# Fused local attention and gMLP on Trainium2: first row tiles remade scaled, an earlier hold in the attention, another order of output rows

## The chip, the cores and the metric

The kernel runs on one core of one Trainium2 chip. The metric is the device time of one execution in microseconds (us): the median of several runs. The engines are named as in the profile: PE is TensorE (matrix products), PEld its weight loads, DVE is VectorE, ACT is ScalarE, POOL is GpSimd, SP is SyncE, which here only issues transfers (DMAs). Each engine works through its own list of instructions in order and waits where an operand isn't ready or a buffer isn't free.

## The reference

With S = 2048 rows and D = 512 columns (batch 1):

```python
xn = layernorm(x)                                   # no scale or shift
# A: 32 heads of 16, each row attends to 8 rows: itself and 7 earlier ones, 2 apart
q, k, v = split(xn @ wqkv)
logits  = einsum(q, k at pos - 2*w for w in 0..7) / 4, masked before row 0
s       = (softmax(logits) weighted sum of v) @ wo
# B: gMLP, F = 1792, Fh = 896
z  = gelu(xn @ w_in)
z1, z2 = z[:, :Fh], layernorm(z[:, Fh:])
g  = w_sp @ z2 + b_sp[:, None]                      # w_sp: 2048 x 2048 over the rows
b  = (z1 * g) @ w_out
out = x + s * silu(b)
```

All is float32. The kernel writes each float32 operand of a product as a high and a low part and sums three products (high x high, high x low, low x high).

## The kernel before

**Layout.** Rows are dealt to NT = 16 row tiles of 128, and these to four chunks of JC = 4 tiles (512 rows). A big buffer, BIG, holds first the planes of xn turned into columns (a high and a low plane for each of four blocks of columns, k = 0 to 3, and each row tile), later z2 and the gated product. To make a high and a low part is called a split: ACT copies the high part (L195), DVE subtracts for the low one (L197).

**Order of the products on PE.** First q, k and v: three groups of columns g = 0, 1, 2 (`product`, L385 to L387), two row tiles at a time (`pair`). ACT moves each result to a staging tile (L433, tile `stage`) and issues its store to a scratch tensor, qkv_d. Then z1 with columns as rows of the result (L687 to L689, tile `z`; weights `w_5h`, `w_lasth` and so on, in the trace), with 7 blocks f by 4 chunks c; ACT applies gelu (L696, tile `z1t`) and stores it. Then z2 (L717 to L719, also tile `z`), gelu at L720 and a layernorm on DVE, POOL and ACT. Then the mixing with w_sp (L812, tile `g`), written as seven block products whose operands are sums of blocks of w_sp and of z2 (the sums L393 are formed on DVE and POOL and kept in sums_d; weights `wsp_0` to `wsp_7` are blocks of w_sp, `ws_0` to `ws_7` such sums; `tr` are transposed tiles of z2 read back from t_d). Then the products with w_out (L1054 to L1056, tile `b`) and with wo (the same lines, tile `s`), and the last arithmetic sg = s * silu(b) + x.

**The rows of the first chunk.** xn of the first four row tiles is only centred when it is put in BIG: their factor 1/std is not known so early. It is applied late: in `pair` and after z2 as the `scale` of ACT's activation (`late_rstd`, which is 1.0 for other tiles), and for z1 on DVE, where chunk c = 0 is multiplied by `rb` (L694), a tile that holds the factors as a row in all partitions. `rows_out` writes means and factors to mv_d, and rb is read from there in the middle of group g = 1, after the weights `wqkv_0` to `wqkv_3` of group 2 have been asked for.

**Raw slots.** Weights, rb and the attention's results that are read back (`ol`) pass through RAW = 4 buffers of one tag. A load into a slot waits until the operations on its last content are through.

**Attention.** It runs on DVE in 32 steps: 16 units, each of four heads (64 columns) and half of the row tiles, and per unit two steps of one chunk each, all kept in one order by `line`. A step multiplies k by q (L565, tile `pr`), sums over the head (L572, tile `lg`), for a unit shifts by the maximum (L587 to L590) and divides by the sum (L601 to L603), then weights v (L609, tile `pv`; `sums_of` lists these 32 operations), folds (L620 on POOL, in the last steps on DVE; L625, L626), transposes (L633, tile `tt`) and stores to o_d from POOL's queue. The scores run three steps ahead of the weighting. k, q and v are read from qkv_d, the first of them by SP's queue, later ones by POOL's. Attention has the lowest priority: a scheduler that lays out each engine's list when the kernel is built puts its steps between other work.

**The hold.** In `plain`, one dependency by hand keeps the weighting of the twelfth step behind the split of weight js = 4 of the first block product. It only orders DVE's list.

**The end.** `load_o` reads four row tiles of attention results for one of the groups, in four parts k, half of each by SP and half by POOL, into raw slots, and splits them (L197; the first group's parts go to BIG, later ones to `o_0` to `o_3`). A group is one chunk; the last four steps of the attention, the 29th to the 32nd, finish the chunks 0, 1, 2 and 3 in this order. The order of chunks in the product with wo is `rows_of` (1, 3, 0, 2).

Of the kernel before, what the change touches and what calls it, by code (L numbers as in the profile page):

```python
# [57 lines left out]
def kernel(  # L58
# [174 lines left out]
        hi, lo = xn_at(j)  # L233
        pin(nc.vector.tensor_tensor(lo, blocks(pt), hi.bitcast(F32), op=ALU.subtract))

    def rows_out(j0, j1):
        turned = const.tile([P, 2 * NT], F32, tag="mvt", name=f"mvt_{j0}", bufs=1)
        pin(nc.vector.transpose(turned, mvx.rearrange("p j a -> p (j a)")))
        for a in range(P // Q):
            pin(nc.sync.dma_start(  # L240
                mv_d[j0:j1, :, a * Q : (a + 1) * Q].rearrange("j a q -> (j a) q"),
                turned[a * Q + 2 * j0 : a * Q + 2 * j1],
            ))
# [51 lines left out]
    def opening(wg):  # L295
        def high(k):
            hi, lo = weight_pair(f"wqkv_0_{k}")
            pin(nc.scalar.activation(hi, raw[k], AF.Copy))
            wg[k] = hi, lo

        def low(k, eng):
            pin(eng.tensor_tensor(wg[k][1], raw[k], wg[k][0].bitcast(F32), op=ALU.subtract))

        left = [12, 12]

        def times(j, *kab):
            for k, a, b in kab:
                pin(nc.tensor.matmul(  # L308
                    first[j], xn_at(j)[a][:, k], wg[k][b],
                    start=left[j] == 12, stop=left[j] == 1,  # L310
                ))
                left[j] -= 1

        x = [load_x(0)]
        raw = [fetch(wqkv[:, 0, 0, :], GC, "wqkv_0_0")]
        x.append(load_x(1))
        raw += [fetch(wqkv[:, 0, k, :], GC, f"wqkv_0_{k}") for k in (1, 2)]
        raw.append(t35("wqkv_0_3r")[:, :GC])
        pin(nc.sync.dma_start(raw[3], wqkv[:, 0, 3, :]))
        x.append(load_x(2))  # L320
        stats_x(0, x[0])
        high(0)
        normal_x(0, x[0])
        low(0, nc.vector)
        p = turned_x(0, x[0])
        stats_x(1, x[1])
        low_x(0, p)
        high(1)
        normal_x(1, x[1])
        rstd_x(0)  # L330
# [12 lines left out]
        normal_x(2, x[2])  # L343
        rstd_x(1)
        first.append(mm("qkv_0_1"))
        times(1, *[(k, 0, 0) for k in range(KB - 1)], (0, 0, 1), (1, 0, 1))
        times(0, (3, 0, 0), (3, 1, 0), (2, 0, 1))
        p = turned_x(2, x[2])
        times(1, (3, 0, 0), *[(k, 1, 0) for k in range(KB)], (2, 0, 1))
        times(0, (3, 0, 1))  # L350
        times(1, (3, 0, 1))
        x += [load_x(j) for j in range(3, OPEN)]
        for j in range(OPEN, OPEN + 4):
            fetch_rows(j)
        raw1 = [fetch(wqkv[:, 1, k, :], GC, f"wqkv_1_{k}") for k in range(3)]
        raw1.append(t2("wqkv_1_3r", 1, tag="tz", bufs=1))
        pin(nc.sync.dma_start(raw1[3], wqkv[:, 1, 3, :]))
        for j in range(3, OPEN):
            xt = x[j]
            stats_x(j, xt)  # L360
            low_x(j - 1, p)
            normal_x(j, xt)
            if j - 1 < JC:
                rstd_x(j - 1)
            first.append(mm(f"qkv_0_{j - 1}"))
            left.append(12)
            times(j - 1, *[(k, 0, i) for i in range(2) for k in range(KB)])
            p = turned_x(j, xt)
            times(j - 1, *[(k, 1, 0) for k in range(KB)])
            row_stats(OPEN + j - 3)  # L370
        low_x(OPEN - 1, p)
        for j in range(10, 13):
            fetch_rows(j)
        for j in range(6, 10):
            fetch_cols(j)
        rows_ready(6, 9)
        rows_out(6, 9)
        return raw1

    def product(g, j, wg):  # L380
# [46 lines left out]
    def pair(g, j0):  # L427
        pins[0] = False
        stage = tmp.tile([P, 2 * GC], F32, tag="t35", name=f"stage_{g}_{j0}", bufs=3)
        sv = stage.rearrange("p (b j c) -> p b j c", b=NBLK, j=2)  # L430
        for j in (j0, j0 + 1):
            pq = first[j] if g == 0 and j < OPEN - 1 else product(g, j, wgs[g])
            nc.scalar.activation(  # L433
                sv[:, :, j % 2, :],
                pq.rearrange("p (b c) -> p b c", b=NBLK),
                AF.Copy,
                scale=late_rstd(j),
            )
        dst = qkv_d[NBLK * g : NBLK * (g + 1), PAD:, :].rearrange(
            "b (p j) c -> p b j c", j=NT  # L440
        )[:, :, j0 : j0 + 2, :]
        nc.scalar.dma_start(dst, sv)
        pins[0] = True
# [10 lines left out]
    rows_ready(9, 13)  # L454
    pair(0, 4)
    column_tile(6)
    rows_out(9, 13)
    column_tile(7)
    low_x(6, cols[6])
    for j in range(10, 12):  # L460
# [6 lines left out]
    column_tile(8)  # L467
    low_x(7, cols[7])
    fetch_cols(12)
    rows_out(13, NT)  # L470
    pair(1, 2)
    column_tile(9)
    low_x(8, cols[8])
# [4 lines left out]
    for j in range(11, NT):  # L478
        if j + 2 < NT:
            fetch_cols(j + 2)  # L480
        turned = column_tile(j)
        if j == 12:
            for i in range(HT - 2):
                pool_sums(1, i, early_tile, turned, SYNC)
        low_x(j - 1, cols[j - 1])
        if j % 2:
            pair(0, j - 5)
    low_x(NT - 1, cols[NT - 1])
    pair(0, 12)
    pair(0, 14)  # L490
    early.__exit__(None, None, None)
    pins[0] = False
    for g in range(1, NG):
        for j in range(OPEN if g == 1 else 0, NT, 2):
            if g == 1 and j == NT // 2:
                pins[0] = True
                wgs[2] = weights(2)
                rows_out(0, JC)
                rb = raws.tile([P, 512], F32, tag="raw", name="rb", bufs=RAW)
                pin(nc.sync.dma_start(  # L500
                    rb.rearrange("p (j q) -> p j q", j=JC),
                    mv_d[:JC, 1].unsqueeze(0).to_broadcast([P, JC, P]),
                ))
            pair(g, j)
            pins[0] = False

# [15 lines left out]
    def attention():  # L522
# [26 lines left out]

        def load_v(u):  # L550
            sub, h = units[u]
            vs[u] = ap_.tile([P, HWIN, CS], F32, tag="v", name=f"v_{sub}_{h}")
            queue = nc.gpsimd if u > 1 else nc.sync
            queue.dma_start(vs[u].rearrange("p r c -> p (r c)"), window(sub, 2, h))

# [94 lines left out]
        for i, (u, j0) in enumerate(steps):  # L650
            coming = steps[i + ahead] if i + ahead < len(steps) else None
            if coming:
                if not coming[1]:
                    start(coming[0])
                pr = scores(*coming)
            if part:
                finish(part)
            if not j0:
                load_v(u)
                normed(u)  # L660
            part = weighted(u, j0)
            if coming:
                heads(*coming, pr)
            first_fold(part, nc.gpsimd if coming else nc.vector)
            if j0 + NJ == NH and u + 1 < len(units):
                exponential(u + 1)
            if coming and coming[1] + NJ == NH:
                shifted(coming[0])
        finish(part)
        tc.cur_priority = saved  # L670

# [7 lines left out]
    for f in range(FB):  # L679
        pair_ = side_pair("w1_last") if f == FB - 1 else None  # L680
        wh, wl = prep(w_in1[:, f, :], KB * P, f"w1_{f}", pair_=pair_)
        for c in range(NC):
# [7 lines left out]
            if c % 2 == 0:  # L690
                zp = t4(f"z1t_{f}_{c}")
            zt = zp[:, c % 2]
            if c == 0:
                nc.vector.tensor_tensor(zt, pz, rb, op=ALU.mult)  # L694
                pz = zt
            nc.scalar.activation(zt, pz, AF.Gelu_apprx_tanh)  # L696
            if c % 2:
                nc.scalar.dma_start(z1_d[f, c - 1 : c + 1].rearrange("c p t -> p c t"), zp)
# [13 lines left out]
    def z2_half(j, h, zt):  # L712
        xh, xl = xn_at(j)
        pz = mm(f"z2_{j}_{h}")[:, : WID[h]]
        for k in range(KB):
# [1 line left out]
            nc.tensor.matmul(pz, xh[:, k], wh, start=k == 0, stop=False)  # L717
            nc.tensor.matmul(pz, xh[:, k], wl, start=False, stop=False)  # L718
            nc.tensor.matmul(pz, xl[:, k], wh, start=False, stop=k == KB - 1)  # L719
        nc.scalar.activation(zt[:, HALF[h]], pz, AF.Gelu_apprx_tanh, scale=late_rstd(j))  # L720

    def spatial_block(c, js):
        return prep(w_sp[c, js], CT, f"wsp_{c}_{js}")
# [43 lines left out]
    for i in range(HT + 2):  # L767
        if i in (1, 3):
            raw_sums(1, HT - 2 + i // 2)
        if i < HT:  # L770
            raw_z[i] = [t4(f"zt_{j}").rearrange("p i t -> p (i t)")[:, :FH] for j in (i, HT + i)]
            for h in range(2):
                for j, zt in zip((i, HT + i), raw_z[i]):
                    z2_half(j, h, zt)
                if i == HT - 1 and h == 0:
                    spatial[0, 1] = spatial_block(0, 1)
        if i == 2:
            b_a = t4("b_a")
            nc.sync.dma_start(
                b_a, b_sp[0:2, :].rearrange("c t -> (c t)").unsqueeze(0).to_broadcast([P, 2 * CT])  # L780
# [66 lines left out]
    def plain(a, c, r):  # L847
        def w(s):
            js = r * HT + s
            pair_ = spatial.get((2 * a + c, js)) or spatial_block(2 * a + c, js)  # L850
            if (a, c, js) == (0, 0, 4):
                tc.add_manual_dep(
                    sums_of[11].ins, lows[-1].ins.name, NOSYNC, reason="first weights ahead"
                )
            return pair_

# [226 lines left out]
    wos = [ut_at(1, f) for f in range(KB)]  # L1083
    for k in range(KB):
        split(*wos[k], fetch(wo[:, k, :], D, f"wo_{k}"))
    rows_of = [c * JC + jj for c in (1, 3, 0, 2) for jj in range(JC)]
    groups = [rows_of[i] // NJ for i in range(0, NT, NJ)]
    fetched = {0: fetch_pair(0)}
    os_ = [load_o(groups[0], k, ut_at(3, k)) for k in range(KB)]
# [70 lines left out]
```

## Time and profile before

| | before |
|---|---|
| time, median of 3 runs (lowest to highest) | 706.84 us (703.7 to 707.46) |
| profiled execution: its own time | 706.57 us |
| its span in the profile | 704.8 us |
| granted TensorE clock, mean | 0.993 |
| PE busy | 689.8 us, 98% |
| DVE busy | 611.2 us, 87% |
| ACT busy | 281.8 us, 40% |
| POOL busy | 224.8 us, 32% |
| chain that ended last | PE 49%, DVE 28%, DMA 11%, issue 8% |

How to read it: the span is what the profile shows of one execution, and the execution's own time has 1.8 us more. Lines such as L694 are lines of the kernel; `z1t<-z,rb` names the tile written and those read, with buffer numbers left out, so that all `z` tiles read alike. In a timeline, a row has its start, its length, engine, line and operation; the bracket at its end is the time for which the engine had been idle and what released it, as inferred from semaphores. The "granted clock" is the share of its full clock that TensorE got.

### The profile page before, as it was taken

Reading aid. Unit: us, or ns where it says so; the run is one execution under the profiler, and the core shown is the slowest. Engines: PE = TensorE matmul, PEld = TensorE weight load, DVE = VectorE, ACT = ScalarE, POOL = GpSimd, SP = SyncE. Lnnn points to the kernel's source line nnn. Section 1 sums busy time; section 2 is a strip of 40 time slices with the busy share of each in tenths; the row PEclk is TensorE's granted clock in tenths of the full one; section 3 lists DMA queues with packets and bytes.
Section 4 is the critical chain, followed back from the end, with each engine's and each line's share of the span. In section 5 each row is a group of like instructions: output and inputs, shape, how many; then the busy total and the mean of one; then the engine's idle time right before and its main releaser. Section 6 shows DMA issues by size and latency. Waiting matters only on the chain.

```text
span 704.8 us, 9222 instructions
## 1 busy us (share of the span) xinstructions
PE 689.8 (98%) x3084; PEld 574.7 (82%) x3084; DVE 611.2 (87%) x886; ACT 281.8 (40%) x458; POOL 224.8 (32%) x242
## 2 busy tenths in 40 slices
PE   8999999999989799999999999999999999999997
PEld 7888888888868688988888878888888888888886
DVE  6774288897999999899998989999999899998266
ACT  4343332331323464696544244532433353311432
POOL 3105485933333244522122311223202102542210
PEclk9999999999999899999999999999999999999999
DMA  8769999879999864448698767757758685453997
GB/s 269 257 194 342 332 361 353 272 223 373 382 371 340 343 207 154 144 147 283 211 365 329 256 231 252 256 160 259 239 169 282 199 270 204 145 169 138 245 340 281
DMA packets 102080, 182.37 MB, mean 259 GB/s; under 512 B 9168, under 2 KB 45264, under 8 KB 102032
## 3 DMA queue, kind: packets, MB, share of 16 engines
q1 hardware_dynamic: 56480, 102.14, 44.0%
q0 software_dynamic: 13824, 52.24, 21.1%
q10 hardware_dynamic: 31728, 27.40, 11.7%
q8 instruction: 24, 0.39, 0.2%
q14 instruction: 24, 0.20, 0.1%
HBM read 122.42 MB, written 59.32 MB: 258 GB/s over the span
## 4 chain that ended last, share of the span: by engine, by line
PE 49%; DVE 28%; DMA 11%; issue 8%; POOL 2%; ACT 1%; SPq 0%; DVEq 0%; ACTq 0%; POOLq 0%
PE g L812 23%; DVE pr L565 5%; DVE lg L572 4%; PE b L1054 4%; PE b L1055 4%; PE b L1056 4%; DVE pv L609 3%; PE qkv L385 2%; PE qkv L387 2%; PE qkv L386 2%; PE s L1054 2%; PE s L1056 2%; PE s L1055 2%; DVE BIG L197 2%; PE qkv L308 2%
## 5 line engine op out<-in xcount | busy, mean ns | idle before, releaser
L620 POOL TENSOR_TENSOR pv<-pv 128x1024 f32<-128x1024 f32 x29 | 70.8, 2441 | 81.7 <-DVE pv L609 81.6
L565 DVE TENSOR_TENSOR pr<-k,q 128x2048 f32<-128x2048 f32 x32 | 76.5, 2392 | 8.7 <-DMA k<-qkv_d 5.2
L609 DVE TENSOR_TENSOR pv<-v,lg 128x2048 f32<-128x2048 f32 x32 | 73.1, 2284 | 1.3 <-DMA v<-qkv_d 0.8
L572 DVE TENSOR_REDUCE lg<-pr 128x128 f32<-128x2048 f32 x32 | 72.9, 2277 | 0.1
L634 POOL DMA_DIRECT2D o_d<-tt x32 | 18.1, 566 | 157.1 <-DVE tt L633 155.0
L433 ACT ACTIVATE stage<-qkv 128x512 f32<-128x512 f32 x36 | 21.4, 595 | 50.1 <-PE qkv L387 44.7
L717 PE MATMUL z<-w_0h,BIG 128*128 128x512 f32 x64 | 26.3, 411 | 4.3 <-DVE lg L587 4.1
L794 POOL DMA_DIRECT2D ol<-o_d x32 | 17.7, 555 | 32.4 <-DVE o_1l L197 8.3
L719 PE MATMUL z<-w_0h,BIG 128*128 128x512 f32 x64 | 26.1, 410 | 0.0
L625 DVE TENSOR_TENSOR pv<-pv 128x512 f32<-128x512 f32 x32 | 24.0, 749 | 2.4 <-POOL pv L620 2.3
L718 PE MATMUL z<-w_0l,BIG 128*128 128x512 f32 x64 | 26.0, 406 | 0.0
L544 POOL DMA_DIRECT2D k<-qkv_d x13 | 7.1, 546 | 55.7 <-DVE pr L565 55.7
L280 DVE TENSOR_TENSOR xT<-xT,mr 128x512 f32<-128x512 f32 x20 | 13.8, 688 | 11.2 <-DMA mr<-mv_d 6.4
L741 ACT ACTIVATE zt<-zt,nmz,mvz 128x896 f32<-128x896 f32 x16 | 17.4, 1130 | 14.2 <-POOL nmz L735 14.1
L393 POOL TENSOR_TENSOR sb<-sa,sb 128x512 f32<-128x512 f32 x12 | 20.1, 1672 | 4.8 <-DMA sb<-in_w_sp 4.5
L719 PE MATMUL z<-w_1h,BIG 128*128 128x384 f32 x64 | 21.5, 336 | 0.0
L717 PE MATMUL z<-w_1h,BIG 128*128 128x384 f32 x64 | 21.5, 336 | 0.0
L718 PE MATMUL z<-w_1l,BIG 128*128 128x384 f32 x64 | 21.4, 335 | 0.0
L729 DVE BATCH_NORM_STATS2 zst<-zt 128x6 f32<-128x448 f32 x32 | 18.8, 604 | 2.8 <-ACT zt L720 2.8
L195 ACT ACTIVATE BIG<-zl 128x512 fp32r<-128x512 f32 x20 | 12.2, 626 | 22.4 <-DVE zl L882 22.4
L696 ACT ACTIVATE z1t<-z 128x512 f32<-128x512 f32 x21 | 12.2, 594 | 21.7 <-DMA z_d<-z1t 19.5
L812 PE MATMUL g<-ws_1h,BIG 128*128 128x512 f32 x52 | 20.4, 391 | 0.3 <-ACT ws_1h L195 0.3
(476 smaller groups left out, 2305.4 us busy)
## 6 DMA issues: line engine op xcount, KB each, us to landing
qkv_d<-stage ACTq DMA_DIRECT2D x24, 512.0 KB
v<-qkv_d POOLq DMA_DIRECT2D x14, 704.0 KB, 5.0
k<-qkv_d POOLq DMA_DIRECT2D x13, 704.0 KB, 6.4
sums_d<-sa POOLq DMA_DIRECT2D x14, 512.0 KB, 7.3
sums_d<-sb POOLq DMA_DIRECT2D x14, 512.0 KB, 7.9
z_d<-z1t ACTq DMA_DIRECT2D x14, 512.0 KB
zl<-z_d SPq DMA_DIRECT2D x12, 512.0 KB
tr<-t_d SPq DMA_DIRECT2D x12, 384.0 KB
```

The source lines that it names most:

```text
L565: line(nc.vector.tensor_tensor(pr, taps(ks[u], j0), qb.unsqueeze(1).to_broadcast([P, W, NJ * CS]), op=ALU.mult))
L572: line(nc.vector.tensor_reduce(lgs[u][:, :, j0 * HS : (j0 + NJ) * HS], pr.rearrange("p w (i d) -> p w i d", d=DH), axis=AX.X, op=ALU.add,))
L609: line(nc.vector.tensor_tensor(pv.rearrange("p w (i d) -> p w i d", d=DH), taps(vs[u], j0).rearrange("p w (i d) -> p w i d", d=DH), lgs[u] ...
L620: eng.tensor_tensor(pv[:, 0:4], pv[:, 0:4], pv[:, 4:8], op=ALU.add)
L625: line(nc.vector.tensor_tensor(pr[:, 0:2], pr[:, 0:2], pr[:, 2:4], op=ALU.add))
L717: nc.tensor.matmul(pz, xh[:, k], wh, start=k == 0, stop=False)
L718: nc.tensor.matmul(pz, xh[:, k], wl, start=False, stop=False)
L719: nc.tensor.matmul(pz, xl[:, k], wh, start=False, stop=k == KB - 1)
L812: nc.tensor.matmul(pg, z[a], w[b], start=start and i == 0, stop=stop and i == 2, skip_group_check=seeded)
L1054: nc.tensor.matmul(pp[:, cols], hi, wh, start=k == 0, stop=False)
L1055: nc.tensor.matmul(pp[:, cols], hi, wl, start=False, stop=False)
L1056: nc.tensor.matmul(pp[:, cols], lo, wh, start=False, stop=k == n - 1)
```

## The change

It has five parts.

1. **Factors out earlier.** `rows_out` takes several ranges of row tiles, and the first four tiles go out with the last three. rb is read at j = 13 of the opening loop, before the weights of group 2 are asked for.
2. **Column tiles remade.** After the last low part of xn, four new chains remake the columns of the first chunk: DVE adds high and low part, multiplies by rb, ACT copies the high part, DVE subtracts for the low part. They use raw slots (tile `xs`). From there on, the first four tiles are like the others: L694 goes, and group 2 and z2 no longer use `late_rstd`.
3. **Two loads.** The load of the bias `b_a` moves from i = 2 to i = 5 of z2's loop. The last v tile takes a buffer of tag k and is loaded when the last scores are done, before the last steps.
4. **The hold.** The tenth step is held, for weight js = 6.
5. **Output rows.** The order of chunks in the product with wo is (1, 0, 2, 3). The product with w_out keeps (1, 3, 0, 2).

```diff
@@ rows_out
-    def rows_out(j0, j1):
+    def rows_out(*spans):
...
-        for a in range(P // Q):
+        for (j0, j1), a in itertools.product(spans, range(P // Q)):
@@ pair
-                scale=late_rstd(j),
+                scale=late_rstd(j) if g < 2 else 1.0,
@@ opening
-    rows_out(13, NT)
+    rows_out((13, NT), (0, JC))
...
     for j in range(11, NT):
...
+        if j == NT - 3:
+            rb = raws.tile([P, 512], F32, tag="raw", name="rb", bufs=RAW)
+            rbv = rb.rearrange("p (j q) -> p j q", j=JC)
+            pin(nc.sync.dma_start(rbv, mv_d[:JC, 1].unsqueeze(0).to_broadcast([P, JC, P])))
...
     low_x(NT - 1, cols[NT - 1])
+    early.__exit__(None, None, None)
+
+    for k in range(KB):
+        hi, lo = [planes[:, FB - KB + k, :JC, a] for a in range(2)]
+        xs = raws.tile([P, 512], F32, tag="raw", name=f"xs_{k}", bufs=RAW)
+        xs = xs.rearrange("p (j q) -> p j q", j=JC)
+        pin(nc.vector.tensor_tensor(xs, hi.bitcast(F32), lo.bitcast(F32), op=ALU.add))
+        pin(nc.vector.tensor_tensor(xs, xs, rbv, op=ALU.mult))
+        pin(nc.scalar.activation(hi, xs, AF.Copy))
+        pin(nc.vector.tensor_tensor(lo, xs, hi.bitcast(F32), op=ALU.subtract))
     pair(0, 12)
     pair(0, 14)
-    early.__exit__(None, None, None)
...
-                rows_out(0, JC)
-                rb = raws.tile([P, 512], F32, tag="raw", name="rb", bufs=RAW)
-                pin(nc.sync.dma_start(
-                    rb.rearrange("p (j q) -> p j q", j=JC),
-                    mv_d[:JC, 1].unsqueeze(0).to_broadcast([P, JC, P]),
-                ))
@@ load_v, and the loop over the steps
-            vs[u] = ap_.tile([P, HWIN, CS], F32, tag="v", name=f"v_{sub}_{h}")
+            vs[u] = ap_.tile([P, HWIN, CS], F32, tag="k" if u == len(units) - 1 else "v", name=f"v_{sub}_{h}")
...
-                load_v(u)
+                if u < len(units) - 1:
+                    load_v(u)
...
+            if i + ahead == len(steps):
+                load_v(len(units) - 1)
@@ z1
-            if c == 0:
-                nc.vector.tensor_tensor(zt, pz, rb, op=ALU.mult)
-                pz = zt
             nc.scalar.activation(zt, pz, AF.Gelu_apprx_tanh)
@@ z2_half
-        nc.scalar.activation(zt[:, HALF[h]], pz, AF.Gelu_apprx_tanh, scale=late_rstd(j))
+        nc.scalar.activation(zt[:, HALF[h]], pz, AF.Gelu_apprx_tanh)
@@ z2's loop
-        if i == 2:
+        if i == 5:
             b_a = t4("b_a")
@@ plain
-            if (a, c, js) == (0, 0, 4):
+            if (a, c, js) == (0, 0, 6):
                 tc.add_manual_dep(
-                    sums_of[11].ins, lows[-1].ins.name, NOSYNC, reason="first weights ahead"
+                    sums_of[9].ins, lows[-1].ins.name, NOSYNC, reason="first weights ahead"
                 )
@@ the product with wo
-    rows_of = [c * JC + jj for c in (1, 3, 0, 2) for jj in range(JC)]
+    rows_of = [c * JC + jj for c in (1, 0, 2, 3) for jj in range(JC)]
```

The scheduler moves many other instructions with these. Three places show what the prediction speaks of. The first is DVE's list at the end of the opening: `xT` and BIG are column tiles of xn, `wqkv_0l` is the low part of a weight of group 2, `pr_0` the first attention operation. Before:

```order
86 L234 TENSOR_TENSOR BIG<-xT_648,BIG 128x4x128
87 L197 TENSOR_TENSOR wqkv_0l<-wqkv_0r,wqkv_0h 128x512
88 L197 TENSOR_TENSOR wqkv_1l<-wqkv_1r,wqkv_1h 128x512
89 L197 TENSOR_TENSOR wqkv_2l<-wqkv_2r,wqkv_2h 128x512
90 L197 TENSOR_TENSOR wqkv_3l<-wqkv_3r,wqkv_3h 128x512
91 L238 STREAM_TRANSPOSE mvt_838<-mvx 128x32
92 L565 TENSOR_TENSOR pr_0_1220<-k_0_1215,q_0_1216 128x2048
```

And after, in the same place (two of the four chains):

```order
86 L234 TENSOR_TENSOR BIG<-xT_652,BIG 128x4x128
87 L499 TENSOR_TENSOR xs_730<-BIG 128x512
88 L500 TENSOR_TENSOR xs_730<-xs_730,rb 128x512
89 L502 TENSOR_TENSOR BIG<-xs_730,BIG 128x4x128
90 L499 TENSOR_TENSOR xs_735<-BIG 128x512
91 L500 TENSOR_TENSOR xs_735<-xs_735,rb 128x512
92 L502 TENSOR_TENSOR BIG<-xs_735,BIG 128x4x128
```

Twelve operations come between the last low part and the splits of wqkv, and the transpose L238 is gone from here. The second place is DVE's list near the end of z1, with the last multiplication by rb (block f = 6, chunk 0). Before:

```order
239 L609 TENSOR_TENSOR pv_0_1421<-v_0_1415,lg_1351 128x2048
240 L572 TENSOR_REDUCE lg_1395<-pr_4_1408 128x8x16
241 L197 TENSOR_TENSOR wsp_0l<-wsp_0r,wsp_0h 128x512
242 L587 MEMSET lg_1395 1x8
243 L587 MEMSET lg_1395 1x16
244 L694 TENSOR_TENSOR z1t_0_2388<-z_6_0_2375,rb 128x512
```

And after:

```order
239 L197 TENSOR_TENSOR wsp_0l<-wsp_0r,wsp_0h 128x512
240 L611 TENSOR_TENSOR lg_1369<-lg_1369,sm_1435 128x256
241 L393 TENSOR_TENSOR sb_5_2296<-sa_5_2295,sb_5_2296 128x512
242 L393 TENSOR_TENSOR sa_5_2295<-sa_5_2295 128x512
243 L393 TENSOR_TENSOR sa_5_2295<-sa_5_2295,sb_5_2296 128x512
244 L617 TENSOR_TENSOR pv_0_1439<-v_0_1433,lg_1369 128x2048
245 L580 TENSOR_REDUCE lg_1413<-pr_4_1426 128x8x16
```

The multiplication is gone, and the first weight of the mixing is split ahead of the weighting of the ninth step. The third place is DVE's list at the hold. Before, the twelfth weighting (`pv`), behind the split of wsp_4; BIG<-zt is z2's split:

```order
364 L197 TENSOR_TENSOR BIG<-zt_2904,BIG 128x4x128
365 L197 TENSOR_TENSOR wsp_3l<-wsp_3r,wsp_3h 128x512
366 L730 BN_AGGR mvz<-zst_3140 128x2
367 L197 TENSOR_TENSOR wsp_4l<-wsp_4r,wsp_4h 128x512
368 L609 TENSOR_TENSOR pv_4_1487<-v_1_1455,lg_1395 128x2048
```

After, the tenth weighting, behind that of wsp_6:

```order
361 L197 TENSOR_TENSOR wsp_4l<-wsp_4r,wsp_4h 128x512
362 L197 TENSOR_TENSOR BIG<-zt_2914,BIG 128x3x128
363 L737 BN_STATS zst_3177<-zt_3084 128x6
364 L738 BN_AGGR mvz<-zst_3173 128x2
365 L197 TENSOR_TENSOR wsp_5l<-wsp_5r,wsp_5h 128x512
366 L197 TENSOR_TENSOR wsp_6l<-wsp_6r,wsp_6h 128x512
367 L617 TENSOR_TENSOR pv_4_1461<-v_0_1433,lg_1369 128x2048
```

At nearly the same place in the list, two steps of the attention fewer have been weighted, and two more weights split.

More of the change, by code (lines that the diff above doesn't have):

```diff
@@ L234, in low_x @@
         pin(nc.vector.tensor_tensor(lo, blocks(pt), hi.bitcast(F32), op=ALU.subtract))
-    def rows_out(j0, j1):
-        turned = const.tile([P, 2 * NT], F32, tag="mvt", name=f"mvt_{j0}", bufs=1)
+    def rows_out(*spans):
+        turned = const.tile([P, 2 * NT], F32, tag="mvt", name=f"mvt_{spans[0][0]}", bufs=1)
         pin(nc.vector.transpose(turned, mvx.rearrange("p j a -> p (j a)")))
-        for a in range(P // Q):
+        for (j0, j1), a in itertools.product(spans, range(P // Q)):
             pin(nc.sync.dma_start(
@@ L376, in opening @@
         rows_ready(6, 9)
-        rows_out(6, 9)
+        rows_out((6, 9))
         return raw1
@@ L456 @@
     column_tile(6)
-    rows_out(9, 13)
+    rows_out((9, 13))
     column_tile(7)
```

## The prediction

> **What bounds the kernel now.** The page comes first: it says whether one engine fills the span.
>
> ```profile
> PE 689.8 (98%) x3084; PEld 574.7 (82%) x3084; DVE 611.2 (87%) x886; ACT 281.8 (40%) x458; POOL 224.8 (32%) x242
> ```
>
> TensorE is busy for 98% of the 704.8 us span, and the change keeps its products, so a gain can only come from the few stretches in which it isn't full. The table of 25-us windows finds them (columns: window, its length, then busy time and count of TensorE, its weight loads, DVE, ACT and POOL, granted clock, DMA share, GB/s).
>
> ```profile
> 200.00:225.00 25.00, 22.32 (x98) 17.82 (x97) 24.86 (x35) 8.86 (x14) 9.08 (x10) 1.00 0.95 347
> 225.00:250.00 25.00, 20.88 (x91) 18.07 (x90) 24.96 (x39) 9.72 (x16) 9.37 (x11) 0.86 0.79 308
> 400.00:425.00 25.00, 23.51 (x101) 18.62 (x100) 20.02 (x32) 11.12 (x19) 3.69 (x3) 1.00 0.73 253
> 425.00:450.00 25.00, 25.00 (x112) 20.69 (x111) 24.45 (x31) 11.20 (x20) 5.10 (x6) 1.00 0.83 267
> ```
>
> A full window holds 112 products, one per 25/112 = 0.223 us. The windows from 200 to 250 us lack time while DVE is full (24.9 of 25) and ACT little over a third busy. TensorE's waits name the partners (in total, times, longest):
>
> ```profile
> PE z L717 <- DVE lg L587: 4.1, 1, 4.1
> PE z L687 <- DVE z1t L694: 2.5, 1, 2.5
> PE g L812 <- DVE ws_1l L197: 0.8, 1, 0.8
> PE g L812 <- DVE ws_3l L197: 0.4, 1, 0.4
> PE z L717 <- DVE z1t L694: 0.2, 1, 0.2
> ```
>
> The longest is put down to a memset of the attention, L587. The timelines of that moment, of TensorE and then of DVE, say otherwise:
>
> ```profile
> 206.05 0.39 PE L689 MATMUL z<-BIG,w_5l 128*128 128x512 f32 x1
> 208.94 0.50 PE L687 MATMUL z<-BIG,w_lasth 128*128 128x512 f32 x1 [2.50 <-DVE z1t L694]
> ...
> 230.99 0.40 PE L718 MATMUL z<-w_0l,BIG 128*128 128x512 f32 x1
> 235.51 0.80 PE L717 MATMUL z<-w_0h,BIG 128*128 128x512 f32 x1 [4.12 <-DVE lg L587]
> ```
> ```profile
> 229.51 2.29 DVE L609 TENSOR_TENSOR pv<-v,lg 128x2048 f32<-128x2048 f32 x1
> 231.71 2.28 DVE L572 TENSOR_REDUCE lg<-pr 128x128 f32<-128x2048 f32 x1
> 233.91 0.93 DVE L197 TENSOR_TENSOR wsp_0l<-wsp_0r,wsp_0h 128x512 fp32r<-128x512 f32 x1
> 234.80 0.66 DVE L694 TENSOR_TENSOR z1t<-z,rb 128x512 f32<-128x512 f32 x1
> ```
>
> The scaling L694 ends at 235.46 and TensorE starts at 235.51: the PSUM tile that L694 reads came free only then. It stood in DVE's list behind two attention operations of 2.3 us and a split. The product after the gap takes 0.80 us against 0.39 to 0.40 before it. The clock around it, in two windows of the same columns:
>
> ```profile
> 227.50:231.50 4.00, 3.89 (x21) 3.32 (x19) 4.00 (x6) 0.23 (x1) 1.26 (x3) 1.00 1.04 384
> 235.50:241.20 5.70, 5.69 (x13) 4.46 (x14) 5.70 (x8) 2.81 (x6) 0.57 (x1) 0.50 1.04 411
> ```
>
> For 5.7 us the granted clock is 0.50, so another 2.85 us is lost behind the gap. Behind the 2.5 us gap the window's clock stays 1.00.
>
> **The change part by part.**
>
> *Scaling taken out of the first product of gMLP.* The groups of L694 and of the activation behind it (min/median/max in ns):
>
> ```profile
> L694 DVE TENSOR_TENSOR z1t<-z,rb x7: 648/678/689, 155.4 to 234.8; 128x512 f32<-128x512 f32 x7
> L696 ACT ACTIVATE z1t<-z x21: 575/597/602, 155.2 to 231.8; 128x512 f32<-128x512 f32 x21
> ```
>
> Seven DVE operations of 0.678 us go: 4.7 us. ACT now empties these banks itself, in 0.60 us each, with no 2.3-us attention operation in its list. On TensorE that gives back, start to start less one product: 208.94 − 206.05 − 0.22 = 2.67; 235.51 − 230.99 − 0.22 = 4.30; the wait of 0.2; the slow clock 2.85. Together 10.0 us. The other end is 0, where ACT is as late as DVE was. I take 10.0, since ACT needs only 8.9 and 9.7 of 25 us in those windows.
>
> The Trainium skill (TensorE: Matmul & The Clock Gate, Part 1) says that the clock is halved after an idle window of about 3.4 us, until a busy window of that length has passed. The trace agrees on the threshold (4.1 us with a drop, 2.5 without) but shows 5.7 us of half clock. By the page's figure the loss would be an estimated 1.7 us, and the time 1.1 us above mine.
>
> *The remade tiles.* Four times three DVE operations and one ACT copy are added behind the last low part, where DVE waits today; the rows are the window, the first operation after DVE's wait, the first attention operation, and TensorE's first use of the third product group's weights.
>
> ```profile
> 50.00:75.00 25.00, 25.00 (x112) 20.72 (x111) 11.21 (x17) 8.70 (x16) 14.11 (x14) 1.00 0.99 324
> 77.63 0.69 DVE L197 TENSOR_TENSOR wqkv_0l<-wqkv_0r,wqkv_0h 128x512 fp32r<-128x512 f32 x1 [11.69 <-ACT wqkv_0h L195]
> 85.40 2.29 DVE L565 TENSOR_TENSOR pr<-k,q 128x2048 f32<-128x2048 f32 x1 [5.16 <-DMA k<-qkv_d]
> 97.48 0.39 PE L385 MATMUL qkv<-wqkv_0h,BIG 128*128 128x512 f32 x1
> ```
>
> Each tile is a chain of three operations of 0.69 and a copy of 0.60, some 2.7 us; four make 10.7 and fill the 11.69 us wait, from 65.9 to 76.6. The wqkv loads now stand on SP behind rb and behind the raw slots that these tiles use, so 1 MB moves while the DMA engines are 0.99 busy: 3.2 us at 324 GB/s alone, two or three times that when shared. Their splits slip from 77.63 to some 83 to 91, and TensorE reads them at 97.48: it pays nothing. The upper end comes from POOL, which forms the sums L393 at that time.
>
> ```profile
> 72.19 1.30 POOL L393 TENSOR_TENSOR sa<-sa 128x512 f32<-128x512 f32 x1
> 98.19 4.02 DVE L565 TENSOR_TENSOR pr<-k,q 128x2048 f32<-128x2048 f32 x1 [1.67 <-DMA q<-qkv_d]
> ```
>
> The operation of 2.29 us took 4.02 at 98.19, beside such sums. If eight of the twelve are held up for 1.30 us each, that is 10.4 us: the splits come by 101 and TensorE loses 3.5. I take 0. The first attention step starts late, for k's load stands behind a store that the four copies delay by 0 to 2.4 us on ACT, and behind that megabyte: 2 to 8 us after 85.40.
>
> The Trainium skill (SBUF — State Buffer, Who interferes with whom) speaks against this place: a DVE instruction with two SBUF inputs is blocked by a GpSimd instruction that reads SBUF and started first, for the whole of it. All twelve have two such inputs; the 4.02 us agrees.
>
> *The hold.* The tenth step's weighting now stands behind the split of wsp_6, where the twelfth stood behind that of wsp_4. The rows are two splits, the held step, and steps 30 and 31 with a split between:
>
> ```profile
> 302.39 0.69 DVE L197 TENSOR_TENSOR wsp_1l<-wsp_1r,wsp_1h 128x512 fp32r<-128x512 f32 x1
> ...
> 306.91 0.64 DVE L197 TENSOR_TENSOR wsp_4l<-wsp_4r,wsp_4h 128x512 fp32r<-128x512 f32 x1
> 307.47 2.28 DVE L609 TENSOR_TENSOR pv<-v,lg 128x2048 f32<-128x2048 f32 x1
> 632.24 2.29 DVE L609 TENSOR_TENSOR pv<-v,lg 128x2048 f32<-128x2048 f32 x1
> 637.01 0.45 DVE L633 STREAM_TRANSPOSE tt<-pv 128x256 f32<-128x256 f32 x1
> 639.62 2.29 DVE L609 TENSOR_TENSOR pv<-v,lg 128x2048 f32<-128x2048 f32 x1 [0.81 <-DMA v<-qkv_d]
> 644.27 0.69 DVE L197 TENSOR_TENSOR BIG<-ol,BIG 128x512 fp32r<-128x512 f32 x1
> ```
>
> A whole step costs DVE about 10 us: 639.62 − 632.24 less the 0.81 wait and a 1.2 us fold that POOL does earlier on, plus the scores' 2.29 and 2.28. Ahead of the hold the list is two steps (20 us) and L694 (4.7) shorter, two splits and norms (some 3) longer, and starts about 5 late: DVE is there near 307 − 17 = 290. What it waits for is paced by TensorE, 10 us earlier than before: 297. So it idles 7 us, and the late start costs nothing more. With L the delay of the thirtieth step's end at 637.46, L = 7 − 4.7 − 0.8 (the last v is loaded ahead) = 1.5; from −5 without the idling, to 8 where the start's delay is not absorbed. TensorE's splits of the mixing stand 20 us of attention earlier, which covers its being 10 us early.
>
> *Mixing, 400 to 425.* 112 − 101 products are 2.5 us, 1.2 of it in the named waits. Loads and splits stand earlier, TensorE comes earlier too: 0 to 2.5, I take 1.0.
>
> *Order of output rows.* The last product takes chunk 1 first; its split ends at 644.27 + 0.69 = 644.96.
>
> ```profile
> 656.45 0.39 PE L1054 MATMUL s<-BIG 128*128 128x512 f32 x1
> 659.31 0.69 DVE L197 TENSOR_TENSOR o_3l<-ol,o_3h 128x512 fp32r<-128x512 f32 x1 [3.34 <-ACT o_3h L195]
> 667.33 0.39 PE L1054 MATMUL s<-BIG,o_0h 128*128 128x512 f32 x1
> ```
>
> That split is read nine products after 656.45, at 658.5: 13.5 us of slack. So the span cannot fall under 704.8 − 13.5 + L = 691.3 + L. Chunk 3, split by 660.0, was read from 667.33 as second; 11 us earlier it would be wanted at 658.4 and stall 1.6. Made last it is wanted 22 us later. In its place chunk 2's last load stands on POOL behind three loads of chunk 3 that wait for raw slots, 0 to 3 us. I take 1.5 for it, and nothing for L, since 691.3 + 1.5 lies under the sum.
>
> *Sum.* 704.8 − 10.0 − 1.0 + 1.5 = 695.3 us of span. The profiled execution's own time, 706.57, is 1.8 over its span and 0.3 under the median of 706.84. That makes 697.1, taken as **697 us**, 1.4% less.
>
> **Rivals.** *The attention becomes the end.* The span is 691.3 + L: with L = 8, 699.3 and a time of 701; with 12, 705. For it: DVE has no room later on (24.96 of 25 us), and two steps are put off. Against: L694 and the wait for v go.
>
> *The hold starves the attention (slower).* wsp_1 to wsp_4 were split from 302.39 to 306.91; if wsp_6 comes not earlier but later, at 314, DVE idles from 290 on for 24 us, L is 24 − 5.5 = 18.5, the span 709.8, and TensorE's wait at the output product, over 4 us long, adds 2.85: 712.7, a time of **714**. It decides from L = 15 on, wsp_6 split after 310. For it: the load waits for raw slots that DVE itself frees. Against: TensorE and ACT, which set z2's pace, come 10 us earlier.
>
> *The wait moves.* ACT stands in order behind its own splits and exponentials, or z2, reached 6 us earlier, waits for its weights. Then 7 to 10 us are lost again: 704 to 707. Against: ACT's 9.72 of 25.
>
> **How the numbers follow.** Forecast 0.57 (694 to 700), attention at the end 0.18 (700 to 705), the wait moves 0.13 (704 to 707), the hold starves 0.12. About 0.5%, 3.5 us, is what a measurement of this kernel can tell from no change: faster is under 703.3, slower over 710.4. Faster: 0.57 + 0.16 + 0.03 = 0.76; same: 0.02 + 0.09 = 0.11; slower: 0.12 and 0.01 of the third. The range begins at 693, with all 2.5 of the mixing back and nothing lost at the end (692.3 and 1.8 are 694.1) and 1 for what two starting gaps hide, and ends at 705, where what is left out is 0.2.
>
> **What would show it.** Right: no z wait at L687 and L717 over 0.5 us, clock 1.00 from 200 to 250, the mixing 10 us earlier, the thirtieth step's end between 632 and 646, no s wait over 3 us. Wrong: a z bank that waits for ACT; a wait for wqkv_0l near 97; DVE idle over 15 us at the hold; s waiting for chunk 1's split.

## The result, and the profile after

The changed kernel took 696.62 us (median of 4 runs, 694.9 to 698.58) beside 707.15 us for the kernel before (703.7 to 709.52): a ratio of 0.9856, with a 95% interval of 0.9807 to 0.9905. Run again beside other kernels it took 698.06 us against 705.19, 0.9915 (0.9881 to 0.9949). Ratios, here and below, are of undisturbed runs alone, so that they differ a little from the ratios of the medians. The forecast was 697. The profiled execution has a span of 695.1 us, 9.7 less than before, and an own time of 696.9.

The page's first line, and the table of windows (columns as in the prediction):

```profile
PE 686.5 (99%) x3084; PEld 572.8 (82%) x3084; DVE 624.6 (90%) x890; ACT 278.0 (40%) x458; POOL 213.9 (31%) x242
```
```profile
200.00:225.00 25.00, 25.00 (x115) 21.07 (x115) 24.69 (x34) 10.56 (x17) 9.53 (x12) 1.00 1.01 377
225.00:250.00 25.00, 25.00 (x125) 22.39 (x125) 23.84 (x43) 6.29 (x12) 8.06 (x13) 1.00 0.77 297
250.00:275.00 25.00, 25.00 (x128) 22.73 (x127) 20.82 (x44) 18.20 (x29) 3.69 (x8) 1.00 0.57 194
275.00:300.00 25.00, 25.00 (x123) 22.11 (x122) 21.57 (x45) 19.52 (x33) 5.56 (x9) 1.00 0.38 130
300.00:325.00 25.00, 23.88 (x105) 19.22 (x105) 23.63 (x30) 16.22 (x27) 8.84 (x9) 1.00 0.69 226
400.00:425.00 25.00, 25.00 (x112) 20.71 (x111) 23.61 (x33) 10.89 (x20) 5.13 (x6) 1.00 0.79 252
```

The two windows from 200 to 250 are full and at full clock, and so is 400 to 425. One new loss of 1.12 us stands in 300 to 325. TensorE's waits after are a short list; those of 1 us and more:

```profile
PE warm L290 <- POOL ident masks.py:199: 1.3, 1, 1.3
PE g L820 <- ACT g L838: 1.1, 1, 1.1
```

No z wait is left (the warm-up is as before). L820 is before's L812; the 1.1 us is ACT seeding a bank with the bias behind a split. On TensorE, the first product with wo and the last:

```profile
645.25 0.39 PE L1062 MATMUL s<-BIG 128*128 128x512 f32 x1
...
689.35 0.28 PE L1064 MATMUL s<-BIG,o_3l 128*128 128x256 f32 x1
```

The product with wo starts at 645.25 instead of 656.45, 11.2 us earlier. Where this was won is read from the first product of z1 and the first of the mixing, before and then after:

```profile
141.00 0.39 PE L687 MATMUL z<-BIG,w_0h 128*128 128x512 f32 x1
304.96 0.39 PE L812 MATMUL g<-wsp_0h,BIG 128*128 128x512 f32 x1
```
```profile
141.11 0.39 PE L698 MATMUL z<-BIG,w_0h 128*128 128x512 f32 x1
294.56 0.39 PE L820 MATMUL g<-wsp_0h,BIG 128*128 128x512 f32 x1
```

z1 and z2 take 153.45 us instead of 163.96, which is 10.5 less: the gaps and the slow clock. The mixing is 0.8 shorter: 2.1 came back at its waits between 400 and 425 (product by product), and 1.3 went at the new wait, from start to start. The opening ends 0.1 later.

TensorE's last product starts 10.65 us earlier than before (700.00), and the span is 9.7 us shorter: 0.55 is lost within these products, in no named wait, and 1.0 behind them. The chain of waits shows the end:

```profile
680.90 6.97 DMA sg<-b_d
...
687.95 1.07 ACT sg L1107
...
689.04 0.70 DVE sg L1117
```

The load of the last rows of b is issued at 680.90 and lands 6.97 us later; silu and the last arithmetic wait for it, not for TensorE.

The start and the hold, on DVE:

```profile
68.23 1.77 DVE L499 TENSOR_TENSOR xs<-BIG 128x512 f32<-128x512 f32 x1
70.03 1.82 DVE L500 TENSOR_TENSOR xs<-xs,rb 128x512 f32<-128x512 f32 x1
72.55 1.14 DVE L502 TENSOR_TENSOR BIG<-xs,BIG 128x512 fp32r<-128x512 f32 x1 [0.70 <-ACT BIG L501]
...
78.99 0.68 DVE L499 TENSOR_TENSOR xs<-BIG 128x512 f32<-128x512 f32 x1
...
85.88 1.00 DVE L502 TENSOR_TENSOR BIG<-xs,BIG 128x512 fp32r<-128x512 f32 x1 [0.70 <-ACT BIG L501]
...
94.08 0.69 DVE L197 TENSOR_TENSOR wqkv_3l<-wqkv_3r,wqkv_3h 128x512 fp32r<-128x512 f32 x1 [3.96 <-ACT wqkv_3h L195]
95.93 2.29 DVE L573 TENSOR_TENSOR pr<-k,q 128x2048 f32<-128x2048 f32 x1 [1.15 <-DMA k<-qkv_d]
...
302.64 2.28 DVE L617 TENSOR_TENSOR pv<-v,lg 128x2048 f32<-128x2048 f32 x1
...
637.57 0.45 DVE L641 STREAM_TRANSPOSE tt<-pv 128x256 f32<-128x256 f32 x1
```

The remade tiles run from 68.23 to 86.88, the last wqkv split ends at 94.77, attention starts at 95.93 (before: 85.40). The tenth step is weighted at 302.64, behind wsp_6. The thirtieth step ends at 638.02: L is 0.56.

### The profile page after: what moved, and what is told of

It reads as the page before. It is cut to its first block, busy times and chain, and to the rows that moved or that the text cites. A ratio compares the mean times of both kernels' runs of the same rounds, so it can differ in the third digit from the quotient of the medians.

```text
span 695.1 us, 9253 instructions
## 1 busy us (share of the span) xinstructions
PE 686.5 (99%) x3084; PEld 572.8 (82%) x3084; DVE 624.6 (90%) x890; ACT 278.0 (40%) x458; POOL 213.9 (31%) x242
## 4 chain that ended last, share of the span: by engine, by line
PE 82%; DMA 6%; DVE 4%; ACT 3%; issue 2%; SPq 1%; POOL 1%; DVEq 0%; ACTq 0%
PE g L820 36%; PE qkv L385 6%; PE qkv L386 6%; PE qkv L387 6%; PE z L699 4%; PE z L698 4%; PE z L700 4%; PE b L1063 3%; PE b L1062 3%; PE b L1064 3%; DMA sg<-b_d 3%; PE z L727 2%; PE z L726 2%; PE z L725 2%; DMA ol<-o_d 2%
## 5 line engine op out<-in xcount | busy, mean ns | idle before, releaser
L617 DVE TENSOR_TENSOR pv<-v,lg 128x2048 f32<-128x2048 f32 x32 | 74.6, 2332 | 1.2 <-DMA v<-qkv_d 0.6
L573 DVE TENSOR_TENSOR pr<-k,q 128x2048 f32<-128x2048 f32 x32 | 73.6, 2300 | 1.3 <-DMA k<-qkv_d 1.1
L433 ACT ACTIVATE stage<-qkv 128x512 f32<-128x512 f32 x40 | 23.0, 591 | 29.7 <-DMA qkv_d<-stage 15.3
L1073 ACT ACTIVATE bt<-b 128x512 f32<-128x512 f32 x16 | 9.4, 597 | 47.0 <-PE b L1064 47.0
L704 ACT ACTIVATE z1t<-z 128x512 f32<-128x512 f32 x28 | 15.5, 596 | 25.7 <-DMA z_d<-z1t 15.1
L727 PE MATMUL z<-w_0h,BIG 128*128 128x512 f32 x64 | 25.1, 391 | 0.0
L725 PE MATMUL z<-w_0h,BIG 128*128 128x512 f32 x64 | 24.9, 389 | 0.0
L728 ACT ACTIVATE zt<-z 128x512 f32<-128x512 f32 (+1 forms) x32 | 15.9, 535 | 15.0 <-DMA sums_d<-sa 12.0
L741 POOL TENSOR_TENSOR mvz<-mvz,nhalf 128x2 f32<-128x2 f32 x8 | 7.5, 937 | 42.6 <-DVE mvz L740 42.6
```

The source lines that it names most:

```text
L573: line(nc.vector.tensor_tensor(pr, taps(ks[u], j0), qb.unsqueeze(1).to_broadcast([P, W, NJ * CS]), op=ALU.mult))
L617: line(nc.vector.tensor_tensor(pv.rearrange("p w (i d) -> p w i d", d=DH), taps(vs[u], j0).rearrange("p w (i d) -> p w i d", d=DH), lgs[u] ...
```

## The experiments

There are three sets of four kernels, each set on another chip, with the kernel before beside it. Its median was 704.16 us (25 runs), 705.19 (28) and 705.06 (15) in the three, and ratios are to these.

**Which part carries the gain.** All four are made from the changed kernel or the one before by exchanging parts.

*scale_only*, the changed kernel with parts 3, 4 and 5 undone (the load of the last v tile too, which is not among the lines shown):

```diff
...
-        if i == 5:
+        if i == 2:
             b_a = t4("b_a")
...
-            if (a, c, js) == (0, 0, 6):
+            if (a, c, js) == (0, 0, 4):
...
-                    sums_of[9].ins, lows[-1].ins.name, NOSYNC, reason="first weights ahead"
+                    sums_of[11].ins, lows[-1].ins.name, NOSYNC, reason="first weights ahead"
...
-    rows_of = [c * JC + jj for c in (1, 0, 2, 3) for jj in range(JC)]
+    rows_of = [c * JC + jj for c in (1, 3, 0, 2) for jj in range(JC)]
```

> The changed kernel with the old hold (twelfth step, weight 4), the old order of output rows and the old loads of b_a and v: only the scaling moves. Theory (the waits for L694 are the gain, but the hold is needed to keep it): the z waits and the slow clock go, 10.0 us, yet two attention steps of about 10 us each again stand ahead of the splits wsp_1 to wsp_7 on DVE, which is idle for only some 8 us between 250 and 300 in the changed kernel. So the first block product waits some 8 to 12 us near 295 to 310, and the time is 702 to 708. Rival (the scaling alone is the whole gain): no g wait over 2 us, 696 to 699. Rival (the last step of chunk 3 decides): a wait of s products over 3 us near 655 to 665.

Measured: 712.71 us, 1.0118 (1.0053 to 1.0182). The scaling alone makes the kernel slower than before, by more than the theory's 702 to 708. The z waits of z1 are gone, but its table of windows and the longest of TensorE's waits show where the time went, at the first products of the mixing:

```profile
275.00:300.00 25.00, 22.71 (x112) 19.72 (x110) 22.17 (x54) 11.06 (x18) 7.17 (x8) 1.00 0.34 114
300.00:325.00 25.00, 17.15 (x62) 12.68 (x63) 23.84 (x37) 17.79 (x30) 6.73 (x11) 0.86 0.59 176
```
```profile
PE g L976 <- ACT zt L725: 6.3, 1, 6.3
```

*rest_only*, the kernel before with the same lines exchanged the other way (parts 3, 4 and 5), and with L694:

> The kernel before with the new hold (tenth step, weight 6), the new order of output rows and the new loads, but with L694 kept. Theory: the waits of z at L687 and L717 and the slow clock stay, 10 us; the mixing wait of 2.5 us goes, since the splits stand earlier: 703.5 to 707. Rival (the hold and the order of rows are the gain, the scaling only makes room): 696 to 700. Rival (the hold starves the attention): a wait of s products for chunk 1 at the end, over 709.

Measured: 706.98 us, 1.0047 (1.0011 to 1.0083). The z waits stay (4.5 and 3.0 us in all), and the mixing is full. So neither half brings anything: with both the ratio is 0.9856 and 0.9915, with one 1.0118 or 1.0047.

*old_hold*, the changed kernel with part 4 alone undone:

> The changed kernel with the old hold alone. Theory: as in the first run of this set, the splits of wsp_1 to wsp_7 come 8 to 12 us later on DVE and TensorE waits for them near 295 to 310; the attention ends earlier in DVE's list, which gains nothing: 703 to 708. Rival (the hold is neutral, since TensorE sets the pace of z2 anyway): 695.5 to 698, no g wait over 2 us.

Measured: 710.22 us, 1.0099 (1.0065 to 1.0133). The hold is what the scaling needs. TensorE's waits of this kernel, the first product behind one of them, and ACT ahead of it:

```profile
PE z L725 <- ACT zt L728: 3.3, 1, 3.3
PE g L820 <- ACT BIG L195: 2.8, 4, 1.2
PE g L979 <- ACT zt L728: 2.3, 1, 2.3
```
```profile
282.56 0.79 PE L725 MATMUL z<-w_0h,BIG 128*128 128x512 f32 x1 [3.32 <-ACT zt L728]
```
```profile
278.50 2.16 ACT L749 ACTIVATE zt<-zt,nmz,mvz 128x896 f32<-128x896 f32 x2 [7.00 <-POOL nmz L743]
```

The wait is not for the splits wsp_1 to wsp_7, as expected, but already in z2: its norms stand on DVE behind the attention, POOL (nmz) gets their result late, ACT waits 7.00 us for POOL and doesn't empty the z banks (L728). The range was missed by 2 us. It counted waits alone, and the slow clock came with them: 0.86 and 0.93 in the two windows from 275 to 325, which is (0.14 + 0.07) x 25 = 5 us.

*old_rows*, the changed kernel with part 5 alone undone:

> The changed kernel with the old order of output rows (1, 3, 0, 2) alone. The prediction's term gives a stall of 1.6 us for chunk 3 as second group: 698. The trace of the changed kernel gives more: the last transpose stands at 665.8, behind the evictions of the first output rows, and chunk 3 would be wanted at 645.25 + 10.9 + 2 = 658.2; with some 4.3 us from transpose to split and an end near 665 to 668 that is a stall of 7 to 10 us, and 2.9 us of slow clock behind a gap over 4 us: 703 to 709. Rival (the order is neutral): 696 to 697.5.

Measured: 699.38 us, 0.9939 (0.9908 to 0.9971), 1.3 us above the changed kernel's second measurement and 2.8 above its first; its interval overlaps that of the second and begins just above the end of that of the first, so the order's worth is not settled. No wait of s products shows, neither the 1.6 of the prediction nor the 7 to 10 of the second reading: with this order TensorE's list puts the four rows' products with o_3 behind those with o_0 to o_2, from 666.73 on. The 2.3 us of its span lie at the end, where the last load of b is issued at 682.13 and takes 8.05 us:

```profile
682.13 8.05 DMA sg<-b_d
690.27 1.06 ACT sg L1107
```

*after_again*, the changed kernel in the second set:

> The changed kernel as it is, so that it stands beside the others on one chip: 696.6 us at the first measurement, 695 to 699 here.

Measured: 698.06 us.

**What L694 itself is worth.** *no_l694*, the kernel before with these lines taken out:

```diff
-            if c == 0:
-                nc.vector.tensor_tensor(zt, pz, rb, op=ALU.mult)
-                pz = zt
```

> The kernel before without L694 (leaves out the factor of the first chunk in z1) and nothing else: the attention starts as early as before, and DVE has 4.7 us less. This tells apart why the scaling with the old hold took 712.7 us. Theory A (the hold must fit TensorE's earlier arrival): the z gaps go, but the list still has the tenth and eleventh steps ahead of z2's norms and the first splits, and TensorE, 10 us earlier, waits for them near 275 to 325: 703 to 711. Rival B (the remade tiles make the attention start 10.5 us late, and that is what the new hold makes good): no gap, 694 to 698.

Measured: 708.37 us, 1.0075 (1.0047 to 1.0103). Theory A: with the attention as early as before, the old hold still loses the gain, to a z wait of 5.6 us and a g wait of 2.8. So the late start that the remade tiles cause is not why the hold is needed.

*no_l694_hold*, the same with the new hold, order of rows and loads:

> The kernel before without L694 (leaves out the factor of the first chunk in z1), with the new hold, order of output rows and loads. It is the changed kernel without the price of the remade tiles. Theory: that price is hidden, so the time is that of the changed kernel, 695 to 698. Rival (the late start of the attention, 10.5 us, costs something at the end): 691 to 694.

Measured: 705.17 us, 1.0000 (0.9966 to 1.0033). Both missed. The z gaps are gone, and a new one stands at the first products of the mixing:

```profile
PE g L812 <- ACT wsp_1h L195: 3.4, 1, 3.4
PE g L812 <- DVE wsp_1l L197: 2.4, 1, 2.4
```

DVE waited 3.37 us for b_a in z2's norms. That this wait keeps the gain away was tried with *no_l694_ba4*:

```diff
-        if i == 5:
+        if i == 4:
             b_a = t4("b_a")
```

> The kernel before without L694 (leaves out the factor of the first chunk in z1), with the new hold, order of output rows and loads, but the bias b_a asked for at i = 4 of z2's loop instead of i = 5: on SP it stands two stores of z2 tiles earlier. With i = 5 this kernel took 705.2 us, and DVE waited 3.4 us for b_a in the middle of z2's norms. Theory (that one load is what kept the gain away): no wait of DVE for b_a, no wait of wsp_1 on TensorE, 695 to 699. Rival (the remade tiles help by another way, such as z2's activation without a scale): 703 to 707, with the same waits near 300.

Measured: 706.13 us, 1.0017 (0.998 to 1.0055). The wait for wsp_1 stays, 4.3 and 2.1 us, but so does DVE's wait for b_a, 3.3 us: the load was issued 8.1 us earlier (272.74 instead of 280.82), and its use stands as much earlier in DVE's list (278.1 instead of 286.1). So this run doesn't take that wait away, and the theory isn't settled by it. Against the theory speaks rest_only, where DVE waits 3.7 us for b_a too and the mixing waits for nothing. In no_l694_ba4 DVE and ACT wait for each other in z2's norms; DVE's waits, then ACT's, of 240 to 310 us:

```profile
DVE BIG L197 <- ACT BIG L195: 9.0, 4, 3.1
DVE b_a L993 <- DMA b_a<-in_b_sp: 3.3, 1, 3.3
```
```profile
ACT BIG L195 <- DVE zt L754: 12.5, 5, 4.6
ACT zt L741 <- POOL nmz L735: 12.4, 7, 6.1
```

In the changed kernel ACT waited 3.4 us for DVE's zt from 250 to 320, and 2.9 in after_again. The lists of DVE and ACT stand in another order in the two kernels. Which difference decides, the remade tiles, z2's activation without a factor, or only the order that the scheduler found, was not told apart.

*l694_back*, the changed kernel with L694 put in again:

> The changed kernel with L694 put back (the factor is applied twice to the first chunk in z1). Theory: the z waits at L687 and L717 come back with it, with or without the slow clock, and DVE has 4.7 us more: 703 to 707. Rival (DVE's list, which now starts its attention later and holds it earlier, has room for L694): 696 to 699.

Measured: 704.94 us, 1.0025 (1.0001 to 1.0048). The waits come back in z1, 5.1 us in two with the slow clock behind the longer, 3.9 us (0.86 from 200 to 225). Two others are new, for the last weight of group 2:

```profile
PE z L698 <- DVE z1t L705: 5.1, 2, 3.9
PE qkv L386 <- DVE wqkv_3l L197: 1.4, 1, 1.4
PE qkv L385 <- ACT wqkv_3h L195: 0.8, 1, 0.8
```

In this kernel's list the split of wqkv_3 stands behind three attention operations and starts at 102.35; in the changed kernel it stands ahead of them, at 94.08. So 2.2 us of this loss don't stand at L694, and the remade tiles are free only while that split keeps its place.

**Three smaller terms.** *old_ba*, the changed kernel with `if i == 2` for b_a:

> The changed kernel with b_a asked for at i = 2, as before. Prediction's term: nothing, 696 to 699. Rival (one buffer of z2's tiles is taken three rounds longer and z2 waits for it): 701 to 706, with waits of z2 products or first weights near 250 to 310.

Measured: 696.06 us, 0.9876 (0.9835 to 0.9917): nothing that the runs can tell, as costed. Its profile lacks the wait for the seed and has a mixing of 273.1 us, where the changed kernel's takes 274.5. The load of the last v tile was not tried alone.

*pool_late*, with POOL's early sums behind the last remade tile:

```diff
-        if j == 12:
-            for i in range(HT - 2):
-                pool_sums(1, i, early_tile, turned, SYNC)
...
+    for i in range(HT - 2):
+        pool_sums(1, i, early_tile, remade, SYNC)
     pair(0, 12)
```

> The changed kernel with POOL's six early sums held until the last remade tile is done, so that POOL forms no sums beside the twelve DVE operations. Theory (they are slow because POOL reads at the same time): each takes 0.69 us instead of up to 2.1, the four chains 11 to 12 us instead of 18.7, and the first attention step starts 5 to 8 us earlier than 95.9; the time stays within 2 us of the changed kernel, 695 to 700, since TensorE doesn't wait there and the hold takes up the difference. Rival (the DMA load or something else slows them): still 1.7 to 2.1 us each.

Measured: 723.55 us, 1.0268 (1.0216 to 1.0319). The first half came as expected. The first chain and the last operation of the fourth, on DVE:

```profile
64.58 0.69 DVE L494 TENSOR_TENSOR xs<-BIG 128x512 f32<-128x512 f32 x1
65.30 0.69 DVE L495 TENSOR_TENSOR xs<-xs,rb 128x512 f32<-128x512 f32 x1
66.69 0.69 DVE L497 TENSOR_TENSOR BIG<-xs,BIG 128x512 fp32r<-128x512 f32 x1 [0.70 <-ACT BIG L496]
...
74.85 0.69 DVE L497 TENSOR_TENSOR BIG<-xs,BIG 128x512 fp32r<-128x512 f32 x1 [0.70 <-ACT BIG L496]
```

The twelve take 0.69 us each and the chains 10.96, where they took up to 2.08 and 18.65 beside POOL's sums; attention starts at 86.39. The time missed by far: the sums, formed and stored later, collide with z1. ACT, which empties the z banks, stands 15.2 us behind the attention's scores and 5.0 us behind the store of a sum, and TensorE waits 23.0 us:

```profile
PE z L696 <- ACT z1t L702: 23.9, 2, 23.0
```

*pace*, the changed kernel with the last fetches of b and x one group earlier:

```diff
-            fetched[i + 4] = fetch_pair(i + 4, arrived[groups[min(i // NJ + 1, 3)]])
+            fetched[i + 4] = fetch_pair(i + 4, arrived[groups[min(i // NJ + 1, 2)]])
```

> The changed kernel with the last two fetches of b and x no longer paced behind the arrival of the last group's attention results, but one group earlier. In the changed kernel the last of these loads is issued at 680.90, lands at 687.87, and the last activation and the last product wait for it: 5.5 us lie between the last product on TensorE and the end, against 4.5 before. Theory: the loads are there in time, and 0.8 to 1.5 us go: a span of 693.5 to 694.5. Rival (the early loads take DMA time from the attention results of chunks 2 and 3): s products wait, 697 to 700.

Measured: 696.78 us, 0.9894 (0.9857 to 0.9931), span 695.1. The last loads are issued at 674.53 and 676.97, and only 4.0 us lie between TensorE's last product and the end, against 5.5 (and 4.8 in after_again). But TensorE ends at 691.2, 0.3 to 1.5 us later. No gain that the runs can tell.

## Why the prediction was right, and where not

**The waits for L694: right, 10.5 us for 10.0.** They and the slow clock are gone (windows 200 to 250), and l694_back brings waits and the slow clock back. ACT as their new owner: no z wait, so "the wait moves" did not happen in z1.

**What the prediction left out: this gain needs the hold.** It said that the splits of the mixing, 20 us of attention earlier in DVE's list, cover TensorE's earlier arrival, and gave the hold only a price. scale_only and old_hold show that without it the gain is lost and 6 to 9 us more, in z2 and the first products of the mixing; in z2 it is the norms that come late, which the prediction did not name. The rival "the wait moves" named z2 as one place where the loss could come back, by its weights; for these kernels the place was right, the mechanism another and its 7 to 10 us too small. That the changed kernel needs the hold is shown by old_hold; no_l694_hold shows that hold and removal together don't suffice in every surrounding, and why is open.

**The remade tiles: the sum right, the sizes wrong.** The chains took 18.65 us, not 10.7, near the upper bound that was worked out from POOL's sums (21.1), and pool_late shows that POOL is the cause. So attention started 10.5 us late, outside the 2 to 8. The changed kernel's own trace says the same and leaves out the other suspect: the third chain ran from 78.99 at 0.68 to 0.69 us each while POOL formed no sum (77.1 to 81.3), although the DMA engines were full then (1.01, against 0.76 in the slow stretches). TensorE paid nothing, as said: the splits of wqkv were through at 94.77, ahead of 97.48. With another list it paid 2.2 us (l694_back), so this is a matter of luck with the list. The Trainium skill (SBUF — State Buffer, Who interferes with whom) predicts this contention for operations with two SBUF inputs beside a GpSimd reader, and the trace agrees: 0.69 us alone, up to 2.08 beside sums of 1.3 to 1.7. That the one which starts first holds the other off isn't shown: the operation of 2.08 us starts at 73.61, ahead of the sum at 73.84.

**The hold: L near, its terms not.** DVE was idle for 4.2 + 3.4 = 7.6 us from 250 to 300 (7 expected), the tenth step stood at 302.64 (297), and the thirtieth ended at L = 0.56 (1.5). But 3.2 us of idle time stood in this stretch before, too:

```profile
250.00:275.00 25.00, 25.00 (x127) 22.62 (x126) 25.00 (x46) 15.88 (x23) 11.74 (x14) 1.00 0.67 220
275.00:300.00 25.00, 25.00 (x124) 22.23 (x123) 21.81 (x51) 12.97 (x23) 9.93 (x10) 1.00 0.42 137
```

From the first attention operation to the thirtieth step's end, DVE works 519.3 us instead of 524.3 and is idle for 22.8 instead of 27.8. So the late start of 10.5 us was made good by 5.0 us of work less (4.7 expected) and by 5.0 us of idle time less, where the sum had 7 more: 4.4 us came from 250 to 300, and more went elsewhere, 6.1 of it from 300 to 450. That the balance came out near 1.5 is in part luck.

**Mixing: near in sum.** Twice the 1.0 came back (2.1), less 1.3 at a new wait for a seed, which the prediction didn't have.

**The end: right in size, wrong in mechanism.** The 1.5 us were lost, but not to chunk 2's load behind chunk 3's: 1.0 of them stand behind the last product, where the load of b is late. In pace, where that load isn't tied to the last group's arrival, this part is 4.0 us instead of 5.5. Nor does the old order of rows stall chunk 3; what it may cost, 1.3 to 2.8 us, shows as a later load of b.

**The rivals.** "The attention becomes the end" and "the hold starves the attention" did not come: L stayed under 1.

## What to carry to other kernels

Taking a wait away on the engine that bounds a kernel makes that engine arrive earlier everywhere after; what other engines prepare for it has to move as far, or the gain is lost a stage later (here 712.7 us with the one half, 707.0 with the other, 696.6 with both, and 704.2 to 707.2 with neither). So cost such an edit together with the order of the lists behind it, and try its halves apart before judging either. Operations added to an engine's idle time cost more than their length alone if a neighbour slows them there (0.69 us alone, up to 2.08 beside POOL's sums): compare both.

## What the runs showed of the hardware that was not expected

The clock falls after shorter gaps than the 4.1 us seen before. In old_hold it falls behind a wait of 3.32 us, in the window from 285 to 290, and in no_l694 behind one of 2.83 us, from 417.0 to 420.6. In old_hold it falls again behind 2.28 and 0.60 us nearly in a row (0.50 from 312.6 to 316.0). In rest_only the window of its 3.0 us wait stays at 1.00:

```profile
285.00:290.00 5.00, 5.00 (x19) 4.32 (x18) 5.00 (x8) 1.39 (x3) 0.00 (x0) 0.63 0.53 202
```
```profile
417.00:420.60 3.60, 3.60 (x10) 2.77 (x10) 3.60 (x8) 0.34 (x1) 0.00 (x0) 0.53 0.91 287
```
```profile
225.00:250.00 25.00, 21.99 (x108) 19.27 (x107) 24.84 (x44) 6.52 (x12) 9.51 (x14) 1.00 0.87 337
```

So the length of a wait alone doesn't tell whether the clock falls, and the threshold that the prediction found to agree with its trace is not borne out by these runs.

And the same program varies more than its first runs told: the kernel before gave 703.7 to 709.52 us in 4 runs, and 698.39 to 706.99 in 24 of 25 others.
